# Decoding two float64 weight arrays: eight wide blocks on VectorE and ScalarE in place of sixteen with GpSimd

## The chip, the cores and the metric

The kernel runs on one core of a Trainium2 chip. The metric is the device time of one execution in microseconds (us); the times below are medians over runs. A core has five instruction streams that matter here: PE (TensorE, matmuls), DVE (VectorE), ACT (ScalarE), POOL (GpSimd) and SP (SyncE, which here only issues transfers). Each works through its own list in order and waits for the others by semaphores.

## The reference

Two attentions with a packed set of 32 keys, a dense layer with SoLU and layer norm, and a layer of eight experts with the best one chosen for each token:

```python
p_packed = sm_attn(p, k, v)               # 8 batches x 8 heads, 576 tokens, 64 wide
out = sm_attn(q, p_packed, p_packed)
h = x @ w_in                              # w_in [512, 1024], float64
solu = h * softmax(h)
ln = layer_norm(solu) * g_ln
x = ln @ w_out                            # w_out [1024, 512], float64
...
```

`w_in` and `w_out` arrive as float64, and everything else as float32. The kernel brings the float64 words to the chip as pairs of 32-bit words and makes float32 values of them there.

## The kernel before

The program has two phases. In the first, each of the 8 batches runs through steps that have a letter in the code: P (`packed`: scores of the packed queries, softmax, packed values), S (`scores2`: the tokens' scores against the packed keys), W (`w_keys`: packed values times `w_in`), A (`attnT`: transposed weights), H (`hidden`: a tile of 128 tokens times 1,024 hidden units, max, exp, mean, variance, norm), T (`lnT`: the normed tile transposed and split into a high and a low part, tiles `lh` and `ll`), X (`second`: times `w_out`) and G (`gate`). The second phase runs the experts. From the second batch on, a fixed list of steps overlaps each batch with its neighbours.

Ahead of that list stands a list written out by hand for the first batch. Into it the decoding is mixed: F issues a transfer of raw words, I decodes a block of `w_in`, D a block of `w_out`. A scheduler then orders each engine's instructions, so the order on an engine is not simply that of the list. W needs all of `w_in`; X needs all of `w_out`.

The arrays are cut into 16 blocks of 512 columns (8 of `w_in`, 8 of `w_out`, 512 KB each). The words lie in pairs, lower word first, so that `hi` and `lo` are each every second 32-bit word. A block takes four or five DVE instructions (lines 114 to 117, and 122 for the two blocks whose flag is "n"), one or two ACT instructions (113, 119) and one or two POOL instructions (120, 123). A block of `w_out` takes two more on ACT (154, 155) and one more on POOL (156). The raw words and the scratch words lie in buffers of later tiles (`room`).

Two chains are spoken of below. In H, the max of a tile (`hm`, line 281) lets ACT write `e` (287), then DVE multiplies `e` by the hidden units (289), and this frees the PSUM buffer `h` for the tile after next; there are two such buffers. `e_2` is `e` of tile 2 of batch 0: its line 289 frees the buffer into which PE puts tile 4, `h_4`. After it, ACT squares (292), POOL takes a power (297), and DVE writes the normed tile (298).

## Time and profile before

| | us |
|---|---|
| median of 3 runs | 968.62 |
| lowest and highest | 967.90, 969.72 |
| span of the profiled execution | 967.9 |
| PE busy | 915.5 (95%) |
| DVE busy | 539.3 (56%) |
| ACT busy | 402.2 (42%) |
| POOL busy | 124.2 (13%) |

The profiled execution's own time is the one of 967.90; its span is the same to a tenth, so nothing lies around it. The median is 0.7 us above it. Busy shares are averages over stages: the shares of single stretches are in the rows further down.

### The profile page before, as it was taken

The page shows a single profiled execution, that of the slowest core. Times are in us where ns is not written, and L with a number is a line of the kernel's source. Part 1 is how long each engine was busy: PE and PEld are TensorE (multiplying, and loading weights), DVE is VectorE, ACT ScalarE, POOL GpSimd, SP SyncE. Part 2 cuts the span into 40 slices and gives each one's busy share as a digit, 9 for nine tenths or more (in the row PEclk, how much of TensorE's full clock was granted, in tenths as well). Part 3 has the DMA queues.
Part 4 walks back from the last instruction along what each step waited for, and adds up shares of the span by engine and source line. Part 5 has one row for each costly group of instructions (what it writes and reads, how often), then busy time and mean ns, then how long its engine had stood idle before and what let it go on. Part 6 is the DMA issues. An engine that isn't in the chain of part 4 may idle for free.

```text
span 967.9 us, 18591 instructions
## 1 busy us (share of the span) xinstructions
PE 915.5 (95%) x7480; PEld 807.3 (83%) x7480; DVE 539.3 (56%) x1090; ACT 402.2 (42%) x800; POOL 124.2 (13%) x228
## 2 busy tenths in 40 slices
PE   4466999999999999999999999999999999999997
PEld 1234777887878878788788999999999999999997
DVE  5999758575575756757456243353434353535331
ACT  4447555444554446444345241333323232324230
POOL 2776312011120101101010000000000000000000
PEclk9988999999999999999999999999999999999999
DMA  9613113022221222200106235353535353433411
GB/s 341 244 45 123 50 56 145 14 90 100 102 98 40 82 82 98 99 2 2 50 1 225 78 116 166 99 175 90 182 99 174 102 173 103 149 127 100 132 46 52
DMA packets 42506, 102.89 MB, mean 106 GB/s; under 512 B 4592, under 2 KB 14384, under 8 KB 38320
## 3 DMA queue, kind: packets, MB, share of 16 engines
q1 hardware_dynamic: 42416, 101.65, 31.1%
q8 instruction: 61, 1.00, 0.4%
q14 instruction: 29, 0.24, 0.1%
HBM read 82.60 MB, written 19.04 MB: 105 GB/s over the span
## 4 chain that ended last, share of the span: by engine, by line
PE 87%; DVE 6%; DMA 2%; ACT 1%; issue 1%; SPq 1%; POOL 0%; DVEq 0%; ACTq 0%
PE y L476 21%; PE x L331 21%; PE h L458 21%; PE h L279 11%; PE lt L315 3%; PE wb L218 2%; PE s L170 2%; PE s L231 2%; PE lg L342 1%; PE pp L193 1%; PE at L260 1%; DMA raw_0a<-w 1%; DVE raw L116 1%; PE a1t L184 1%; DVE e L298 1%
## 5 line engine op out<-in xcount | busy, mean ns | idle before, releaser
L331 PE MATMUL x<-lh,wo_hi 128*128 128x320 f32 (+1 forms) x512 | 155.8, 304 | 0.2 <-ACT x L333 0.2
L331 PE MATMUL x<-lh,wo_lo 128*128 128x320 f32 (+1 forms) x512 | 152.5, 298 | 0.0
L331 PE MATMUL x<-ll,wo_hi 128*128 128x320 f32 (+1 forms) x512 | 152.4, 298 | 0.0
L331 PEld LDWEIGHTS x<-lh,wo_hi 128*128 128x128 f32 x512 | 96.7, 189 | 18.6 <-issue 7.4
L331 PEld LDWEIGHTS x<-ll,wo_hi 128*128 128x128 f32 x512 | 96.9, 189 | 3.9 <-issue 2.5
L331 PEld LDWEIGHTS x<-lh,wo_lo 128*128 128x128 f32 x512 | 96.8, 189 | 2.2 <-issue 0.8
L318 DVE TENSOR_TENSOR ll<-lt,lh 128x512 fp32r<-128x512 f32 (+1 forms) x80 | 50.5, 632 | 47.7 <-ACT lh L317 47.6
L279 PE MATMUL h<-wbh,ath 128*128 128x512 f32 (+1 forms) x160 | 68.3, 429 | 6.6 <-DVE e L289 5.9
L281 DVE TENSOR_REDUCE hm<-h 128x1 f32<-128x512 f32 (+1 forms) x80 | 54.3, 685 | 26.2 <-PE h L279 25.7
L279 PE MATMUL h<-wbh,atl 128*128 128x512 f32 (+1 forms) x160 | 65.2, 408 | 0.0
L279 PE MATMUL h<-wbl,ath 128*128 128x512 f32 (+1 forms) x160 | 64.6, 404 | 0.0
L317 ACT CAST lh<-lt 128x512 fp32r<-128x512 f32 (+1 forms) x80 | 43.1, 540 | 46.4 <-PE lt L315 45.8
L489 DVE TENSOR_TENSOR o<-y,gb 128x576 f32<-128x576 f32 (+1 forms) x33 | 24.4, 739 | 67.7 <-PE y L476 65.6
L289 DVE SCALAR_TENSOR_TENSOR e<-e,h 128x1024 f32<-128x1024 f32 (+1 forms) x40 | 48.6, 1215 | 19.9 <-ACT e L287 19.9
L292 ACT ACTIVATE sq<-e,mu 128x1024 bf16<-128x1024 f32 (+1 forms) x40 | 46.0, 1150 | 22.1 <-DVE e L289 17.0
L287 ACT ACTIVATE e<-h,hm 128x1024 f32<-128x1024 f32 (+1 forms) x40 | 44.6, 1115 | 24.8 <-DVE hm L282 24.5
L333 ACT COPY x<-x 128x256 f32<-128x256 f32 (+1 forms) x64 | 25.4, 397 | 62.4 <-PE x L331 62.2
L315 PE MATMUL lt<-ident,e 128*128 128x128 f32 (+1 forms) x320 | 48.5, 271 | 0.9 <-DVE ll L318 0.9
L464 DVE SCALAR_TENSOR_TENSOR hl<-h,hh 128x576 fp32r<-128x576 f32 x64 | 47.8, 749 | 0.3 <-ACT hh L463 0.2
L315 PEld LDWEIGHTS lt<-ident,e 128*128 128x128 f32 (+1 forms) x320 | 35.9, 142 | 9.1 <-issue 4.4
L279 PEld LDWEIGHTS h<-wbh,ath 128*128 128x128 f32 (+1 forms) x160 | 29.8, 186 | 15.5 <-DVE e L289 7.1
L298 DVE TENSOR_SCALAR e<-e,mu,va 128x1024 f32<-128x1024 f32 (+1 forms) x40 | 35.3, 882 | 11.3 <-POOL va L297 10.5
(239 smaller groups left out, 2172.5 us busy)
## 6 DMA issues: line engine op xcount, KB each, us to landing
k<-kT SPq DMA_DIRECT2D x16, 576.0 KB
q<-qT SPq DMA_DIRECT2D x8, 1152.0 KB
x2s<-x SPq DMA_DIRECT2D x8, 1152.0 KB
x<-x2s SPq DMA_DIRECT2D x8, 1152.0 KB
yT<-o SPq DMA_DIRECT2D x31, 288.0 KB
v<-vm SPq DMA_DIRECT2D x8, 1024.0 KB
raw<-w_in SPq DMA_DIRECT2D x8, 512.0 KB
raw<-w_out SPq DMA_DIRECT2D x8, 512.0 KB
```

The source lines that it names most:

```text
L279: T.matmul(ps[:rows, cols], s[x][:, t, g, :rows], s[y][:, g, cols], start=(n == 0), stop=(n == len(passes) - 1))
L281: V.tensor_reduce(nm[:rows, hf : hf + 1], ps[:rows, cols], axis=AX.X, op=ALU.max, negate=True)
L287: A.activation(er, psr, AF.Exp, bias=nm[:rows, 0:1], accum_out=z[:rows])
L289: V.scalar_tensor_tensor(er, er, 1.0 / FF, psr, op0=ALU.mult, op1=ALU.mult, accum_out=mu[:rows])
L292: A.activation(sq[:rows], er, AF.Square, bias=mu[:rows], scale=-float(FF), accum_out=va[:rows])
L298: V.tensor_scalar(er, er, mu[:rows], va[:rows], op0=ALU.add, op1=ALU.mult)
L315: T.transpose(ps[:, fc, :rows], e[:rows, (f0 + fc) * P : (f0 + fc + 1) * P], ident[:rows, :rows])
L318: V.tensor_sub(s["ll", part][:, f0 : f0 + 4, t0 - p0 : t0 - p0 + rows], ps[:, :, :rows], f32(hi))
L331: T.matmul(ps[:, :pn], w[:, fc, cols], s[x, part][:, fc, :], start=(n == 0), stop=(n == 3 * NF - 1))
L458: T.matmul(ps[:, hf, :HALF], w[:, dc, :], x[:, dc, hf * HALF : (hf + 1) * HALF], start=(n == 0), stop=(n == 3 * NC - 1))
L464: V.scalar_tensor_tensor(lo, ps[:, :, :HALF], 0.0, f32(hi), op0=ALU.max, op1=ALU.subtract)
L476: T.matmul(ps[:, hf, :HALF], w[:, fc % 4, :], x[fc][:, hf, :], start=(n == 0), stop=(n == 3 * NF - 1))
```

## The change

Each array is cut into 4 blocks of twice the columns (1,024 columns, 1 MB each): 8 blocks in all. A value is now made as a power of two, taken from the top 16-bit word and left in bfloat16, times the mantissa as a number. A block takes five DVE instructions and one ACT instruction, and a block of `w_out` two ACT scalings, one ACT cast and one DVE subtraction (line 150) more. POOL takes no part. The decoding is done in place in the raw words, with a small 16-bit tile `pw` (two buffers) beside it. The raw words of the first two blocks lie in the buffers of `wbh` and `wbl`, the others in those of `lh`, `ll` and `x2`. The hand-written list is new too.

```diff
-        room = "lh0 ll0 lh1 ll1 e e x2 lh0 ll0 lh1 ll1 e lh1 ll1 x2 lh1".split()
-        by_pool = "yyyyyyyyyynyynyy"
+        room = "wbh wbl lh0 ll0 lh1 ll1 x2 lh1".split()
...
-            lo, hi = w[:, :, 0], w[:, :, 1]
-            a, b2 = t[:, 0], t[:, 1]
-            A.activation(f32(a), f32(hi), AF.Abs)
-            V.tensor_scalar(f32(a), f32(a), F64_LEAST, None, op0=ALU.max)
-            V.tensor_scalar(b2, a, 3, 0x3FFFFFFF, op0=ALU.logical_shift_left, op1=ALU.bitwise_and)
-            V.scalar_tensor_tensor(a, hi, -0x40000000, b2, op0=ALU.bitwise_and, op1=ALU.bitwise_or)
-            V.tensor_scalar(b2, a, -0x800000, None, op0=ALU.bitwise_and)
-            if through_pool:
-                A.activation(f32(lo), lo.bitcast(U32), AF.Copy, scale=2.0**-52)
-                G.tensor_tensor(f32(b2), f32(lo), f32(b2), op=ALU.mult)
-            else:
-                V.scalar_tensor_tensor(f32(b2), lo.bitcast(U32), 2.0**-52, f32(b2), op0=ALU.mult, op1=ALU.mult)
-            G.tensor_tensor(dst, f32(a), f32(b2), op=ALU.add)
+            w = raw.rearrange("p (n w) -> p n w", w=2)
             lo, hi = w[:, :, 0], w[:, :, 1]
+            top = raw.bitcast(U16).rearrange("p (n w) -> p n w", w=4)[:, :, 3]
+            t = p2.tile([P, FF], U16, name=f"pw{i}", tag="pw")
+            V.tensor_scalar(t, top, 0x7FF0, None, op0=ALU.bitwise_and)
+            A.activation(t, t, AF.Relu, bias=mexp, scale=8.0)
+            V.scalar_tensor_tensor(t, top, 0x8000, t, op0=ALU.bitwise_and, op1=ALU.bitwise_or)
+            V.tensor_scalar(hi, hi, 0xFFFFF, 0x100000, op0=ALU.bitwise_and, op1=ALU.bitwise_or)
+            V.scalar_tensor_tensor(f32(lo), lo.bitcast(U32), 2.0**-32, hi, op0=ALU.mult, op1=ALU.add)
+            dst = f32(hi) if dst is None else dst
+            V.scalar_tensor_tensor(dst, f32(lo), 2.0**-20, t.bitcast(BF16), op0=ALU.mult, op1=ALU.mult)
+            return dst
...
-            G.tensor_tensor(wo_lo[:, fc, :], raw, f32(wo_hi[:, fc, :]), op=ALU.subtract)
+            V.tensor_sub(wo_lo[:, 2 * i : 2 * i + 2, :], w, f32(wo_hi[:, 2 * i : 2 * i + 2, :]))
...
-        for step in ("K F0 V F1 F4 F2 F3 F5 P S1 S0 I1 F8 S2 F6 I6 F10 F9 F7 I0 I3 I2 I4 F13 F11 C0 L+ I5 I7 "
-                     "W F12 A0 F14 A1 A2 D0 F15 D1 D2 D3 D4 D5 D7 D6 C1").split():
+        for step in ("K F0 F1 V F2 F3 C0 F4 F5 F6 P S0 S1 S2 I0 I1 I2 I3 W F7 A0 L+ H0 H1 D0 D1 T0 T1 D2 D3 A1 A2 C1").split():
```

SP's list (the transfers) at its start, before: the raw words of one block (`raw<-w_in`) stand ahead of the values and queries of batch 0 (`v`, `q`).

```order
L132 DMA k_130<-kT 128x4x288 x2
L105 DMA raw_133<-w_in 128x512
L138 DMA v_135<-vm 128x2048
L139 DMA v_135<-vt 64x512
L140 DMA q_136<-qT 128x2304
L105 DMA raw_140<-w_in 128x512
```

SP's list at the same place, of the change:

```order
L127 DMA k_132<-kT 128x4x288 x2
L98 DMA raw_135<-w_in 128x1024
L98 DMA raw_137<-w_in 128x1024
L133 DMA v_139<-vm 128x2048
L134 DMA v_139<-vt 64x512
L135 DMA q_140<-qT 128x2304
L98 DMA raw_144<-w_in 128x1024
```

Ahead of `v` and `q` now stand two blocks of twice the size.

DVE's list while the first blocks of `w_in` are decoded, before (`raw` and `bits` are a block's words and scratch, `pn` the packed values of batch 0):

```order
L114 TENSOR_SCALAR bits_143<-bits_143 128x512
L117 TENSOR_SCALAR raw_140<-raw_140 128x512
L115 TENSOR_SCALAR bits_143<-bits_143 128x512
L116 SCALAR_TENSOR_TENSOR bits_143<-raw_142,bits_143 128x512
L114 TENSOR_SCALAR raw_145<-raw_145 128x512
L117 TENSOR_SCALAR bits_143<-bits_143 128x512
L115 TENSOR_SCALAR raw_145<-raw_145 128x512
L114 TENSOR_SCALAR raw_147<-raw_147 128x512
L116 SCALAR_TENSOR_TENSOR raw_145<-raw_145 128x512
L196 TENSOR_TENSOR pn_253<-pp_212,rz_152 128x128
```

DVE's list at the same place, of the change (L111, L113, L114, L115 and L117 are the five DVE lines of the new `decode`, top to bottom):

```order
L113 SCALAR_TENSOR_TENSOR pw_341<-raw_137,pw_341 128x1024
L117 SCALAR_TENSOR_TENSOR w_in_sb<-raw_135,pw_334 128x1024
L168 TENSOR_TENSOR nm_1_187<-nm_1_187 128x1
L114 TENSOR_SCALAR raw_137<-raw_137 128x1024
L115 SCALAR_TENSOR_TENSOR raw_137<-raw_137 128x1024
L174 SCALAR_TENSOR_TENSOR z_1_202<-z_1_202 128x1
L117 SCALAR_TENSOR_TENSOR w_in_sb<-raw_137,pw_341 128x1024
L175 RECIPROCAL rz_156<-z_1_202 128x1
L111 TENSOR_SCALAR pw_348<-raw_144 128x1024
L113 SCALAR_TENSOR_TENSOR pw_348<-raw_144,pw_348 128x1024
L190 TENSOR_TENSOR pn_257<-pp_216,rz_156 128x128
```

Most of the new decode rows take two tensors, and L111 of a block is here followed at once by its L113, between which ACT has to work.

DVE's list up to `e_2`, before; the last of the 16 blocks (`raw_489`) stands right ahead of it:

```order
L298 TENSOR_SCALAR e_1_811<-e_1_811,mu_1_814,va_1_816 128x1024
L282 TENSOR_TENSOR hm_2_842<-hm_2_842 128x1
L281 TENSOR_REDUCE hm_3_873<-h_3_872 128x1
L114 TENSOR_SCALAR raw_489<-raw_489 128x512
L282 TENSOR_TENSOR hm_3_873<-hm_3_873 128x1
L115 TENSOR_SCALAR raw_489<-raw_489 128x512
L116 SCALAR_TENSOR_TENSOR raw_489<-raw_489 128x512
L117 TENSOR_SCALAR raw_489<-raw_489 128x512
L289 SCALAR_TENSOR_TENSOR e_2_858,mu_2_861<-e_2_858,h_2_841 128x1024
L318 TENSOR_TENSOR ll_0_826<-lt_0_0_827,lh_0_825 128x4x128
```

DVE's list up to the same instruction, of the change, where it is on L283:

```order
L150 TENSOR_TENSOR wo_lo<-raw_392,wo_hi 128x1024
...
L312 TENSOR_TENSOR ll_0_499<-lt_0_0_500,lh_0_498 128x4x128
L168 TENSOR_TENSOR nm_1_594<-nm_1_594 128x1
L312 TENSOR_TENSOR ll_0_499<-lt_0_4_507,lh_0_498 128x4x128
L275 TENSOR_REDUCE hm_2_753<-h_2_752 128x1
L174 SCALAR_TENSOR_TENSOR z_1_609<-z_1_609 128x1
L276 TENSOR_TENSOR hm_2_753<-hm_2_753 128x1
L175 RECIPROCAL rz_563<-z_1_609 128x1
L275 TENSOR_REDUCE hm_3_784<-h_3_783 128x1
L276 TENSOR_TENSOR hm_3_784<-hm_3_784 128x1
L283 SCALAR_TENSOR_TENSOR e_2_769,mu_2_772<-e_2_769,h_2_752 128x1024
```

All decode rows still stand ahead of `e_2`, the last of them (L150) 15 rows ahead; two rows of `ll_0` (L312, before L318) have moved to its front. On PE, the packed values of batch 1 (`pp`) have moved behind the first half of `h_4`, and the transposes of tile 1 (`lt_1`) to its front. From the middle of the third batch's W step on, the orders of all engines are the same as before.

## Rows read from the trace of the kernel before

**Rows 1.** Windows: length; busy of PE, PEld, DVE, ACT, POOL; clock; DMA share, GB/s.

```profile
0.00:10.00 10.00, 2.37 (x16) 0.43 (x16) 2.78 (x18) 2.98 (x5) 0.68 (x6) 1.00 0.78 275
10.00:20.00 10.00, 6.94 (x94) 3.84 (x98) 5.71 (x17) 6.36 (x18) 3.05 (x3) 1.00 1.02 392
20.00:90.00 70.00, 38.05 (x317) 22.58 (x306) 67.56 (x112) 37.97 (x76) 51.83 (x44) 0.94 0.44 151
90.00:100.00 10.00, 9.49 (x95) 7.31 (x96) 8.91 (x20) 7.31 (x14) 7.22 (x12) 0.72 0.23 94
110.00:200.00 90.00, 89.75 (x781) 70.50 (x780) 56.42 (x131) 44.94 (x100) 12.13 (x33) 1.00 0.21 69
```

**Rows 2.** The chain of waits, in order of time: start, us, what.

```profile
2.56 6.03 DMA raw<-w_in
...
89.32 1.15 DVE e L289 x2
...
90.51 2.82 PE h L279 x6
```

**Rows 3.** Windows of tiles `raw` and `bits` alone, and the group in both.

```profile
9.00:90.00 81.00, 40.97 (x57) 17.94 (x30) 34.93 (x25) 0.95 0.52 185
...
9.00:90.00 81.00, 9.24 (x12) 2.07 (x3) 8.13 (x6) 0.95 0.52 185
...
L116 DVE SCALAR_TENSOR_TENSOR bits<-raw,bits 128x512 int32<-128x512 int32 x3 | 3.2, 1064 | 0.0
```

**Rows 4.** Timeline of DVE and POOL: start, us, engine, line.

```profile
9.30 0.43 DVE L114 TENSOR_SCALAR raw<-raw 128x512 f32<-128x512 f32 x1 [0.18 <-ACT raw L113]
...
19.75 1.68 DVE L116 SCALAR_TENSOR_TENSOR bits<-raw,bits 128x512 int32<-128x512 int32 x1
...
27.07 0.41 DVE L117 TENSOR_SCALAR raw<-raw 128x512 int32<-128x512 int32 x1
27.40 0.68 DVE L116 SCALAR_TENSOR_TENSOR raw<-raw 128x512 int32<-128x512 int32 x1
...
19.51 1.37 POOL L120 TENSOR_TENSOR raw<-raw 128x512 f32<-128x512 f32 x1 [5.35 <-DVE raw L117]
```

**Rows 5.** Wide DVE work: a group of the whole kernel; line 298 after 110 us, min/median/max.

```profile
L289 DVE SCALAR_TENSOR_TENSOR e<-e,h 128x1024 f32<-128x1024 f32 x32 | 38.9, 1217 | 17.5 <-ACT e L287 17.5
...
L298 DVE TENSOR_SCALAR e<-e,mu,va x35: 794/812/816, 134.0 to 521.1; 128x1024 f32<-128x1024 f32 x28, 64x1024 f32<-64x1024 f32 x7
```

**Rows 6.** Timeline of DVE, rows outside the decoding.

```profile
46.78 0.94 DVE L243 TENSOR_SCALAR z<-z 128x16 f32<-128x16 f32 x1
...
48.08 1.01 DVE L243 TENSOR_SCALAR z<-z 64x8 f32<-64x8 f32 x1
...
71.06 0.15 DVE L282 TENSOR_TENSOR hm<-hm 128x1 f32<-128x1 f32 x1
...
73.65 1.25 DVE L282 TENSOR_TENSOR hm<-hm 128x1 f32<-128x1 f32 x1
...
81.73 1.64 DVE L298 TENSOR_SCALAR e<-e,mu,va 128x1024 f32<-128x1024 f32 x1
...
84.04 1.55 DVE L298 TENSOR_SCALAR e<-e,mu,va 128x1024 f32<-128x1024 f32 x1
```

**Rows 7.** Two groups up to 110 and 100 us, and a row of DVE's timeline.

```profile
L245 POOL TENSOR_TENSOR a<-a,z 128x512 f32<-128x512 f32 x4 | 4.4, 1089 | 3.2 <-PE wb L218 1.9 <-DVE z L244 1.3
...
L318 DVE TENSOR_TENSOR ll<-lt,lh 128x512 fp32r<-128x512 f32 x4 | 2.7, 687 | 0.7 <-ACT lh L317 0.7
...
49.72 1.16 DVE L115 TENSOR_SCALAR raw<-raw 128x512 int32<-128x512 int32 x1
```

**Rows 8.** Timeline of ACT and PE.

```profile
71.24 1.12 ACT L287 ACTIVATE e<-h,hm 128x1024 f32<-128x1024 f32 x1 [1.37 <-DVE hm L282]
...
84.12 1.04 PE L315 MATMUL lt<-ident,e 128*128 128x128 f32 x8
...
85.97 1.73 PE L193 MATMUL pp<-v,a1T 128*32 128x64 f32 x80 [0.80 <-ACT a1T L185]
```

More of the change, by code (lines that the diff above doesn't have):

```diff
@@ L57, in fused_kernel @@
     V.memset(mhalf, -0.5)
+    mexp = const.tile([P, 1], F32, name="mexp")
+    V.memset(mexp, -8.0 * 16 * 896)
     eidx = const.tile([1, B], I32, name="eidx")
@@ L108, in decode @@
[L108 to L123 removed]
+            pool = pa if room[i][0] == "w" else p1
@@ new lines, in fetch, with decode @@
+            raw = pool.tile([P, 2 * FF], I32, name=f"raw{i}", tag=room[i])
+            SY.dma_start(raw.bitcast(I64) if len(src.shape) == 2 else raw.bitcast(I64).rearrange("p (f n) -> p f n", f=src.shape[1]), src)
+            return raw
+        def decode(i, raw, dst):
+            w = raw.rearrange("p (n w) -> p n w", w=2)
+            lo, hi = w[:, :, 0], w[:, :, 1]
+            top = raw.bitcast(U16).rearrange("p (n w) -> p n w", w=4)[:, :, 3]
[8 more added lines that the diff above has]
+            return dst
@@ L144, in load, with decode_w_in, decode_w_out @@
             load_vq(b)
[L146 to L156 removed]
+        def decode_w_in(c, raw):
+            decode(c, raw, w_in_sb[:, c, :])
+        def decode_w_out(i, raw):
+            w = decode(4 + i, raw, None).rearrange("p (f n) -> p f n", f=2)
+            for k in range(2):
+                fc = 2 * i + k
+                A.activation(w[:, k], w[:, k], AF.Copy, scale=g_sb[:, fc : fc + 1])
+            A.copy(wo_hi[:, 2 * i : 2 * i + 2, :], w)
+            V.tensor_sub(wo_lo[:, 2 * i : 2 * i + 2, :], w, f32(wo_hi[:, 2 * i : 2 * i + 2, :]))
         def packed(b):
```

28 lines of the change are left out of this document (3 added, 25 removed).

## The prediction

> **What bounds the kernel now.** I read the windows first. From 110 to 200 us PE is busy 89.75 of 90 us, so once it has come that far only less work could help it. From 20 to 90 us it is busy 38.05 of 70, and DVE 67.56 of 70 [rows 1]: there DVE's list, in its fixed order, sets the pace. PE's idle time up to 90 us is 90 - 2.37 - 6.94 - 38.05 = 42.6 us. The chain of waits shows where this ends: line 289 of `e_2` is done at about 90.5, and at 90.51 PE starts `h_4`, for which that row freed the buffer [rows 2]. From there PE is 9.49 of 10 us busy. So I ask one thing: how much earlier does DVE reach the end of `e_2`? PE's work behind it is the same but for some steps moved across, and the orders soon are the same, so the end of the kernel moves with it.
>
> Then I looked at what DVE does there. All 66 decode rows stand ahead of `e_2`. In the windows of the tiles they take 40.97 + 9.24 - 3.2 = 47.0 us (3.2 us lie in both) [rows 3]. Much of it isn't work: line 116 takes 0.68 us at 27.40 and 1.68 at 19.75, where POOL has had a multiply running since 19.51 for 1.37 us [rows 4]. Such a row of DVE ends only once POOL is through. Rows that aren't decoding suffer too: line 282, 0.15 us at 71.06, takes 1.25 at 73.65 [rows 6].
>
> **The change, term by term,** in DVE time up to the end of `e_2`, start to start (a row overlaps the next by 0.07: 27.07 + 0.41 is 27.48, and the next starts at 27.40 [rows 4]).
>
> 1. Removed: 66 rows, 47.0 us, in which their overlaps with one another are already out. For their overlaps with other rows I take 0.05 a row, 3.3 in all: -43.7.
>
> 2. Added: 44 rows, all ahead of `e_2`: 8 x 5, and 4 subtractions (line 150) that POOL did before. 24 rows take two tensors (lines 113, 115, 117), as line 289 does at the same width for 1.217 us [rows 5]; so do the 4 subtractions: 28 x 1.217 = 34.1. 16 rows take one tensor (lines 111, 114). At 512 columns such a row takes 0.41 against 0.68 with two tensors [rows 4], though its fixed part must be as large: two columns at a time. From 512 to 1,024 columns two-tensor rows grow by 1.217 - 0.68 = 0.54, so these should grow by 0.27 to 0.68: 16 x 0.68 = 10.9. With overlaps out, 45.0 - 44 x 0.07 = 41.9: +41.9. Line 298, one tensor wide with two column operands, takes 0.81 [rows 5], which would add 2.1. No row shows a one-tensor row on every second word or every fourth half word, as lines 111 and 114 read; bounds are 0.41 (half the width) and 1.217 (one column at a time). I take 0.68, because line 116, which reads `hi` at every second word, at 0.68 loses nothing against row groups on dense words (0.687, line 318 [rows 7]).
>
> The Trainium skill (Vector Engine (DVE) Microarchitecture Reference, 5.1 Performance modes) names no step as a condition for running one-tensor rows two at a time between SBUF tiles; by it lines 111 and 114 stay at the dense rate, which gives the sum that I use. The same page (5.2 Measured stream behaviour on trn2) speaks against this change: a port keeps its rate only on runs of two adjacent words, and a source that hops at every word cost 1.73 instead of 1.05 ns a column there. By that figure 24 two-tensor rows would take 0.73 us more each, an estimate of +17.5 us; line 116 at 0.68 does not bear it out for one such input.
>
> 3. Delays that POOL's decode work put on other rows: line 298 of `e_0` and `e_1` 1.64 and 1.55 instead of 0.81, two rows of line 282 about 1.25 instead of 0.15, one of line 243 0.94 instead of 0.15 [rows 5, 6]: 0.83 + 0.74 + 2.2 + 0.79 = 4.6. I leave out smaller ones: -4.4, start to start.
>
> 4. Delays that stay: POOL's three softmax multiplies (1.09 us [rows 7]). Before, one met line 243 (1.01 at 48.08 [rows 6], 0.85 lost), and one a decode row (1.16 at 49.72 [rows 7], in term 1). Now nearly every row between is a decode row of the kind that waits, so all three are paid: 3 x 1.05 - 0.85 = +2.3.
>
> 5. Two rows of `ll_0` (0.687 [rows 7]) now stand ahead of `e_2`: +1.2.
>
> 6. Start: the first block, 512 KB asked for at 2.56, is there after 6.03 us, at 8.6 [rows 2], and DVE's first decode row starts at 9.30, after an ACT row [rows 4]. A block of 1 MB takes 512 KB / 392 GB/s [rows 1] = 1.3 us longer, but DVE needs no ACT first: first row at 9.95, +0.65. That two blocks stand ahead of `v` and `q` makes these some 4 us later; `v` is needed only after two softmaxes, and DVE has block 1 to decode meanwhile: nothing on the path.
>
> 7. Idle time of DVE: before, 4.29 from 10 to 20 and 2.44 from 20 to 90 [rows 1], 6.7. Now: twice a block's line 113 stands right behind its line 111 with ACT's row between (1.12 at this width, as line 287 [rows 8], and 0.15 for the two handovers), 2.5. After `e_0` most decode work is gone, and DVE waits for PE, ACT and POOL in turn: I reckon 2.5, what 20 to 90 us had. 5.0 in all: -1.7.
>
> Up to `e_2`: -43.7 + 41.9 - 4.4 + 2.3 + 1.2 + 0.65 - 1.7 = -3.75.
>
> 8. PE behind that point: `pp` of batch 1 (1.73) now stands behind the first half of `h_4`, and the eight transposes of tile 1 (1.04) in front [rows 8]: +0.7. DVE has no more POOL delays from 90 to 100 us, where PE idled 0.51 [rows 1]: -0.5. The granted clock was 0.72 there [rows 1], part of the time at 1.2 GHz after a wait of PE; PE waits in the same way ahead of `h_4` now, so I leave it: 0.
>
> Costs of nothing: ACT loses far more than it gains and was busy 37.97 of 70 us [rows 1], which hides its rows. The last block's transfer (`raw_392`) waits on SP for line 150 of the block whose buffer it takes, and behind it stand the keys of batch 2, needed only in that batch's first step. DVE's line 111 for it stands seven rows behind that line 150: about 6 us against 2.7 of transfer and the issue. If that cover fails, DVE stands still for the difference, a microsecond or two.
>
> Sum: -3.75 + 0.7 - 0.5 = -3.55, so 967.9 - 3.55 = 964.35 for an execution like the profiled one; the median of the runs shown is 0.7 above it: **965.0 us**.
>
> **Rivals.**
> - *One column at a time* (slower). If lines 111 and 114 lose the double rate on strided words, 16 rows cost 1.217 instead of 0.68: +8.6, 973.6. For it: no row shows a stepped one-tensor row. Against: line 116's unhurt step. It turns the sign above 0.68 + 3.55/16 = 0.90 us a row.
> - *Three stepped streams* (slower). Line 115 reads `lo` and `hi` and writes `lo`, all at every second word; line 116 had one stream like it. At half rate its eight rows cost 1.07 us more each (1,024 columns at 1.04 ns): +8.5, 973.5. If all 24 two-tensor rows ran at half rate, it would be +25.7. (It is what the Trainium skill says in 5.2 of the page named above, in the one place where the rows leave room for it.)
> - *Nothing shows.* DVE is relieved, but between `e_0` and `e_2` the chain through PE's `h_2`, ACT and POOL sets the pace, and DVE only idles more: 968.6. For it: after `e_0` only one decode row is left in DVE's list. Against: DVE idled 2.44 us in 70 [rows 1].
> - *More than the sum.* Adding the new list row by row from 9.95, with its waits, brings me to `e_2` at 84 to 85 instead of 90.5; and if PE comes to `h_4` at 2.4 GHz, the 10 x (1 - 0.72) = 2.8 us that the lower clock cost from 90 to 100 [rows 1] are saved too: 968.6 - 5.5 - 2.8, about 960.5.
>
> **How the numbers follow.** No change means within 0.2% (1.9 us), about what a measurement of this kernel can tell: 966.7 to 970.6. The sum's case has 0.48 (own range 961.5 to 968.5; 0.38 of it faster, 0.10 same), more than the sum 0.12 (faster), nothing shows 0.14 (same), one column at a time 0.12 and three stepped streams 0.14, of which 0.02 ends within the bounds. So faster 0.50, same 0.26, slower 0.24. The range goes from 959.5 to 974.0: below it lies some of the fourth rival, above it the far form of the second and what comes with either, some 0.15 together.
>
> **What would show it.** Lines 111 and 114 near 0.68 us, lines 113, 115 and 117 near 1.2. POOL nearly empty from 10 to 90 us. Line 282 and line 298's successors without rows over 1 us but beside the three softmax multiplies. `e_2` done at about 86.7 and PE busy from there. Wrong would make it: wide rows far above 1.2 us, long DVE idle between 10 and 35 us (transfers or ACT), or DVE idle after `e_0` of 5 us and more.

## The result, and the profile after

The changed kernel takes 957.05 us (median of 4 runs, 956.84 to 957.72), the one before 968.26 on the same chip (4 runs, 967.7 to 969.72): a ratio of 0.9878, 95% interval 0.9865 to 0.9892. It is 1.2% faster, by more than three times what the prediction said (11.9 us between the two profiled spans, 967.9 and 956.0, against 3.55), and the median lies below the predicted range.

One number of the prediction's base needs a word. In the changed kernel's profiled execution 1.7 us lie around the span (957.72 against 956.0), and it is nearly so in every run below; the profiled execution before was therefore more likely the one of 969.72 than that of 967.90. The forecast of the median stays where it was (969.72 - 3.55 - 1.1 = 965.1), and from here on spans are compared with spans.

The windows of the changed kernel, the stretches of [rows 1]: length; busy of PE, PEld, DVE, ACT, POOL with their instructions; clock; DMA share, GB/s. The last row is DVE alone, from its first decode row to the end of `e_2`.

```profile
10.00:20.00 10.00, 3.97 (x24) 1.66 (x24) 8.80 (x14) 4.40 (x10) 0.00 (x0) 1.00 1.02 391
20.00:90.00 70.00, 48.30 (x419) 30.38 (x419) 65.26 (x109) 38.57 (x69) 13.60 (x19) 0.78 0.45 163
90.00:100.00 10.00, 10.00 (x133) 8.76 (x132) 9.35 (x22) 6.12 (x13) 2.13 (x5) 1.00 0.24 72
...
10.19:82.77 72.58, 68.24 (x111) 0.79 0.53 196
```

The same window of DVE alone in the kernel before, up to its own end of `e_2`:

```profile
9.30:90.51 81.21, 74.44 (x131) 0.95 0.52 185
```

From 20 to 90 us POOL is busy 13.60 us instead of 51.83 and PE 48.30 instead of 38.05 (in part because its clock there is 0.78 and not 0.94: the same matmul is busy for longer); DVE is nearly as full as it was, 65.26 instead of 67.56. Its list up to `e_2` takes 72.58 us instead of 81.21, with 68.24 busy instead of 74.44 in 111 instructions instead of 131. From 90 to 100 us PE has no idle time and a clock of 1.00, where before it was 9.49 busy at 0.72 [rows 1].

The chain of waits around the end of `e_2`: start, us, what.

```profile
70.97 4.73 PE h L273 x12
...
77.83 2.77 PE h L273 x12
...
80.63 0.70 DVE hm L275
...
81.51 1.22 DVE e L283 x2
82.73 0.04 issue
82.77 1.59 PE h L273 x6
84.37 1.66 PE pp L187 x80
86.03 0.67 PE x L325 x4
```

The place is the one that the prediction names, DVE's last row of `e_2` and behind it `h_4`, but it comes at 82.77 instead of 90.51 [rows 2], and PE does the first six matmuls of `h_4` in 1.59 us, which took 2.82. The same view shows the two levels of the clock: twelve matmuls of a tile take 4.73 us at 70.97, behind a long wait of PE, and 2.77 at 77.83. The first X matmul, behind `h_4`'s first half and `pp`, starts at about 86 us (85.96); before it started at 99.23. PE's timeline of the changed kernel and of the one before:

```profile
85.96 0.38 PE L325 MATMUL x<-lh,wo_hi 128*128 128x256 f32 x1
...
99.23 0.36 PE L331 MATMUL x<-lh,wo_hi 128*128 128x256 f32 x1
```

One thing more stands in this chain: the matmuls of `h_2` (70.97) and `h_3` (77.83) are right ahead of DVE's last rows, and DVE waits for `h_3`. Its timeline:

```profile
80.63 0.69 DVE L275 TENSOR_REDUCE hm<-h 128x1 f32<-128x512 f32 x1 [0.30 <-PE h L273]
```

So from about 71 us on DVE's list is not alone in setting the pace.

DVE's groups from 9 to 91 us: line, operation, tiles, shapes, count; busy, mean ns; idle time ahead and what ended it.

```profile
L115 DVE SCALAR_TENSOR_TENSOR raw<-raw 128x1024 f32<-128x1024 uint32 x8 | 9.7, 1214 | 0.1
L113 DVE SCALAR_TENSOR_TENSOR pw<-raw,pw 128x1024 uint16<-128x1024 uint16 x8 | 9.7, 1207 | 2.2 <-ACT pw L112 2.2
L114 DVE TENSOR_SCALAR raw<-raw 128x1024 int32<-128x1024 int32 x8 | 5.4, 681 | 0.0
L111 DVE TENSOR_SCALAR pw<-raw 128x1024 uint16<-128x1024 uint16 x8 | 5.4, 681 | 1.0 <-DMA raw<-w_in 1.0
...
L117 DVE SCALAR_TENSOR_TENSOR w_in_sb<-raw,pw 128x1024 f32<-128x1024 f32 x4 | 4.9, 1218 | 0.0
L150 DVE TENSOR_TENSOR wo_lo<-raw,wo_hi 128x1024 fp32r<-128x1024 f32 x4 | 4.8, 1208 | 0.0
...
L292 DVE TENSOR_SCALAR e<-e,mu,va 128x1024 f32<-128x1024 f32 x4 | 3.2, 812 | 1.4 <-POOL va L291 1.4
```

One-tensor rows on every second word (L114) and every fourth half word (L111) take 0.681 us; two-tensor rows take 1.21, also L115 with all its streams at every second word. L292, whose two ahead of `e_2` took 1.64 and 1.55 [rows 6], is at 0.81.

Rows of the changed kernel's timeline: start, us, engine, line, tiles, and the idle time ahead in brackets.

```profile
42.94 1.00 DVE L237 TENSOR_SCALAR z<-z 128x16 f32<-128x16 f32 x1
...
47.23 0.92 DVE L237 TENSOR_SCALAR z<-z 64x8 f32<-64x8 f32 x1
...
42.08 1.83 POOL L239 TENSOR_TENSOR a<-a,z 128x512 f32<-128x512 f32 x1 [40.78 <-DVE z L238]
46.90 1.22 POOL L239 TENSOR_TENSOR a<-a,z 128x512 f32<-128x512 f32 x1 [2.99 <-DVE z L238]
50.13 4.29 POOL L239 TENSOR_TENSOR a<-a,z 64x256 f32<-64x256 f32 x1 [2.01 <-ACT pw L112]
...
82.77 0.45 PE L273 MATMUL h<-wbh,ath 128*64 128x512 f32 x1 [0.76 <-DVE e L283]
83.06 0.39 PE L273 MATMUL h<-wbl,ath 128*64 128x512 f32 x1
...
101.53 1.09 PE L212 MATMUL wb<-w_in_sb,ppc 64*32 64x512 f32 x16
```

And of the kernel before, the first two matmuls of `h_4` (the second answers to the one at 83.06) and one of the four groups of eight for batch 1, two of which stand as one row at 101.53 above:

```profile
90.51 0.69 PE L279 MATMUL h<-wbh,ath 128*64 128x512 f32 x1 [2.81 <-DVE e L289]
91.00 0.63 PE L279 MATMUL h<-wbl,ath 128*64 128x512 f32 x1
...
104.19 1.06 PE L218 MATMUL wb<-w_in_sb,ppc 64*32 64x512 f32 x8
```

The only two DVE rows outside the decoding that POOL still stretches are the two of L237. POOL's own multiplies are the stretched ones now: 4.29 us for the smallest of them. PE waits 0.76 us ahead of `h_4` instead of 2.81, and comes to it at 2.4 GHz.

### The profile page after: what moved, and what is told of

The parts are those of the page before. It is cut to its first block, busy times and chain, and to the rows that moved or that the text cites. A ratio compares the mean times of both kernels' runs of the same rounds, so it can differ in the third digit from the quotient of the medians.

```text
span 956.0 us, 18453 instructions
## 1 busy us (share of the span) xinstructions
PE 911.4 (95%) x7480; PEld 806.0 (84%) x7480; DVE 531.5 (56%) x1069; ACT 393.0 (41%) x774; POOL 74.3 (8%) x190
## 4 chain that ended last, share of the span: by engine, by line
PE 89%; DVE 6%; DMA 2%; ACT 1%; issue 1%; SPq 0%; ACTq 0%; DVEq 0%
PE x L325 22%; PE y L468 21%; PE h L450 21%; PE h L273 11%; PE lt L309 3%; PE wb L212 2%; PE s L225 2%; PE lg L336 2%; PE s L164 2%; PE pp L187 1%; PE at L254 1%; DVE raw L115 1%; DVE pw L113 1%; DMA raw<-w_in 1%; DMA raw_0a<-w 1%
## 5 line engine op out<-in xcount | busy, mean ns | idle before, releaser
L312 DVE TENSOR_TENSOR ll<-lt,lh 128x512 fp32r<-128x512 f32 (+1 forms) x80 | 50.4, 631 | 43.1 <-ACT lh L311 43.0
L283 DVE SCALAR_TENSOR_TENSOR e<-e,h 128x1024 f32<-128x1024 f32 (+1 forms) x40 | 48.6, 1216 | 21.1 <-ACT e L281 21.1
L455 ACT ACTIVATE hh<-h 128x576 fp32r<-128x576 f32 x64 | 41.3, 647 | 0.0
L292 DVE TENSOR_SCALAR e<-e,mu,va 128x1024 f32<-128x1024 f32 (+1 forms) x40 | 32.3, 807 | 11.1 <-POOL va L291 10.4
```

What stands on the lines that cost most here:

```text
L283: V.scalar_tensor_tensor(er, er, 1.0 / FF, psr, op0=ALU.mult, op1=ALU.mult, accum_out=mu[:rows])
L312: V.tensor_sub(s["ll", part][:, f0 : f0 + 4, t0 - p0 : t0 - p0 + rows], ps[:, :, :rows], f32(hi))
```

## The experiments

"Pinned" below means that every instruction of an engine is chained to the one ahead of it, so that the scheduler can't choose another order (`order` lists the instructions, engine by engine):

```diff
+        for k in order:
+            if k != 65535 and last is not None:
+                tc.add_manual_dep(seq[k], seq[last].name, mybir.DependencyInfo(mybir.DependencyClass.NoSync, mybir.DependencyReason.DATA))
+            last = None if k == 65535 else int(k)
```

Several kernels that were not pinned came out in an order of their own; where that decides the reading, it is said. Ratios are against the kernel before on the same chip, whose median was between 969.2 and 969.5 in these sets.

### The kernel before without POOL, and without POOL's work

```diff
-        by_pool = "yyyyyyyyyynyynyy"
+        by_pool = "n" * 16
...
-            G.tensor_tensor(dst, f32(a), f32(b2), op=ALU.add)
+            V.tensor_tensor(dst, f32(a), f32(b2), op=ALU.add)
...
-            G.tensor_tensor(wo_lo[:, fc, :], raw, f32(wo_hi[:, fc, :]), op=ALU.subtract)
+            V.tensor_sub(wo_lo[:, fc, :], raw, f32(wo_hi[:, fc, :]))
```

> The kernel before with GpSimd taken off its decode work and nothing else: 16 blocks of 512 columns, the old arithmetic; the 16 additions, the 14 products that GpSimd did and the 8 subtractions now stand in DVE's list. My theory: POOL's rows cost DVE waiting time, and it is the shorter arithmetic together with POOL's absence that brings the gain, neither of them alone. In the trace of before, 66 decode rows take 48.5 us, 17.7 more than the same rows at the shortest duration of their form, and other rows 3.7 more: 21.4 us of waiting to be freed. Added are 38 two-tensor rows of 512 columns, 0.68 - 0.07 = 0.61 each: 23.2 us. So the end of e_2 stays within 3 us of 90.5 and the kernel at 965 to 972 us. Rival, that POOL's removal is the gain by itself: e_2 near 83, some 958 to 961 us.

964.33 us (963.37 to 964.53), ratio 0.9952, interval 0.9935 to 0.9969. `e_2` is done at 90.2, as before: all but two of DVE's 104 decode rows stand ahead of it, so DVE does nearly all of POOL's work in the time in which it waited for POOL. Yet the kernel is faster, just below the range expected, and PE's list came out otherwise. Its timeline:

```profile
87.92 0.38 PE L331 MATMUL x<-lh,wo_hi 128*128 128x256 f32 x1 [1.03 <-DVE ll L318]
...
90.26 0.45 PE L279 MATMUL h<-wbh,ath 128*64 128x512 f32 x1
```

X work fills what was PE's wait, and `h_4` comes without a wait and at 2.4 GHz (0.29 us from its first matmul to the next at 90.55, before 0.49). The end of `e_2` alone does not give the time.

Next, POOL's product, sum and subtraction left out, with copies on ACT so that all else stays (what is lost of the weights is the lower word's part, and the low half of `w_out`; the number that sends the experts into further passes is held at 0):

```diff
-                G.tensor_tensor(f32(b2), f32(lo), f32(b2), op=ALU.mult)
...
-            G.tensor_tensor(dst, f32(a), f32(b2), op=ALU.add)
+            if dst is not None:
+                A.copy(dst, f32(a))
...
-            G.tensor_tensor(wo_lo[:, fc, :], raw, f32(wo_hi[:, fc, :]), op=ALU.subtract)
```

> The kernel before with POOL's decode work left out and DVE's 66 decode rows kept: the product with the mantissa, the addition and the subtraction for wo_lo are not computed (ACT copies the word with sign and exponent instead, wo_lo is zero, and the loop over the remaining experts is held at no pass). Theory: DVE's rows fall to their unhurt durations, 0.41 for lines with one tensor and 0.68 for those with two; the decode rows' sum falls from 48.5 to about 31 us, and e_2 ends 15 to 20 us earlier unless PE's and ACT's chain from h_0 to e_2 sets the pace first: 948 to 956 us. Rival, that the stretched rows of before had another cause (the steps of two words, the transfers): the sum stays above 42 us and the time at 962 to 970.

956.4 us (955.97 to 957.81), ratio 0.9878, interval 0.9862 to 0.9895, just above the range expected. With the same DVE rows `e_2` is done at 72.6, 18 us earlier: about what the 66 decode rows of the kernel before take above the shortest of their form (17.7 of their 48.5 us). So POOL's work held DVE's decoding up by 18 us. The total gains 13.7 in the span and not 18: behind X, PE idles 3.2 us from 110 to 300 us here, where it idled 0.55 before, in an order that differs up to batch 5.

### POOL beside the new decoding

Twelve products on POOL that nobody reads, behind the first three blocks of `w_in`; all other engines' orders are those of the changed kernel, row for row.

```diff
-            decode(c, raw, w_in_sb[:, c, :])
+            decode(c, raw, w_in_sb[:, c, :]); [G.tensor_tensor(scr, w_in_sb[:, c, :512], w_in_sb[:, c, 512:], op=ALU.mult) for _ in range(4 if c < 3 else 0)]
```

> The changed kernel with twelve products of 128 x 512 added on POOL, four behind each of the first three blocks of w_in, into a tile that nobody reads; DVE's order is the same, row for row. POOL alone needs 12 x 1.09 = 13.1 us for them, beside the decode rows from about 18.6 us on. Theory, that DVE's two-tensor rows keep the path and only one-tensor rows wait: the rows of lines 111 and 114 beside them grow, those of lines 113, 115 and 117 stay below 1.3, POOL's rows take 2 us and more, DVE loses 1 to 3 us in all: 957 to 960 us. Rival, that POOL holds DVE up as in the kernel before, 0.39 us per us of POOL or more, or one whole row each: DVE loses 5 to 13 us, 962 to 970 us.

966.26 us (9 runs, 965.56 to 967.25), ratio 0.9971, interval 0.9961 to 0.9981; span 964.6, 8.6 above the changed kernel's. The timeline of POOL and DVE:

```profile
18.85 14.76 POOL L142 TENSOR_TENSOR scr<-w_in_sb 128x512 f32<-128x512 f32 x8 [17.55 <-DVE nm L168]
...
19.47 2.17 DVE L115 SCALAR_TENSOR_TENSOR raw<-raw 128x1024 f32<-128x1024 uint32 x1
21.57 1.23 DVE L174 SCALAR_TENSOR_TENSOR z<-z 128x1 f32<-128x1 f32 x1
22.71 1.21 DVE L117 SCALAR_TENSOR_TENSOR w_in_sb<-raw,pw 128x1024 f32<-128x1024 f32 x1
...
23.92 1.68 DVE L111 TENSOR_SCALAR pw<-raw 128x1024 uint16<-128x1024 uint16 x1
```

Each side waits for the other. A POOL row takes 14.76 / 8 = 1.85 us instead of 1.09 [rows 7]; of DVE, L115 loses 0.96, a row of one column (L174) 1.08, L117 then nothing, L111 1.0. `e_2` comes 9.1 us later (91.8) and X 9.1 later (95.05): 0.76 us of DVE for each of the twelve rows, passed on to the end but for 0.5 us. The theory that a two-tensor row keeps its way beside POOL falls (L115).

### One part of the change undone: the subtractions on POOL

```diff
-            V.tensor_sub(wo_lo[:, 2 * i : 2 * i + 2, :], w, f32(wo_hi[:, 2 * i : 2 * i + 2, :]))
+            G.tensor_tensor(wo_lo[:, 2 * i : 2 * i + 2, :], w, f32(wo_hi[:, 2 * i : 2 * i + 2, :]), op=ALU.subtract)
```

> The changed kernel with one part undone: the four subtractions for wo_lo (128 x 1024) go back to POOL. DVE loses four rows of 1.21 - 0.07, 4.6 us ahead of e_2. Theory, that DVE's two-tensor rows, one close behind the other, keep the path and POOL waits: POOL's rows take 2.5 to 5 us, DVE's others lose 1 to 2 us in all, e_2 ends 2 to 4 us earlier, 953 to 956 us. Rival, that POOL holds DVE up as it did before (0.39 us of DVE for each us of POOL's rows, or the whole row where DVE comes second): four rows of 2.2 us cost DVE 3.5 to 8 us, e_2 at the same place or later, 956 to 961 us.

967.1 us (10 runs, 965.97 to 968.45), ratio 0.9982, interval 0.9973 to 0.9992. It says little by itself, since the scheduler gave another order up to batch 4: `e_2` is done at 82.9 and X starts at 84.87, no later than in the changed kernel, and the time goes behind that. The window from 150 to 200 us:

```profile
150.00:200.00 50.00, 47.84 (x388) 36.40 (x387) 32.39 (x79) 24.25 (x54) 6.91 (x17) 0.93 0.19 65
```

PE idles 2.2 us there, and its clock is 0.93. So the same edit again, the other engines pinned to the changed kernel's order:

> The four subtractions for wo_lo on POOL once more, now with every engine's order pinned to that of the changed kernel (each row is chained to the one ahead of it, POOL's as in the first such run), since the run without pins came out with another order up to batch 4. DVE has four rows of 1.14 us less ahead of e_2, 4.6 us. Theory, that the first run lost its time by its order behind batch 0 and not by POOL: POOL's rows of 2.2 to 3 us cost DVE 3 to 6 us, so e_2 ends within 1.5 us of 82.7 and the kernel takes 955 to 959 us. Rival, that POOL's four rows themselves cost the 10 us: 963 to 968 us again.

962.9 us (961.61 to 964.52), ratio 0.9933, interval 0.9917 to 0.995; span 961.2, 5.2 above the changed kernel's and between the two ranges expected. `e_2` is done at 86.7, 4.0 later, though DVE has four rows fewer (4.6 us); X starts at 91.29. DVE and POOL in the timeline:

```profile
48.74 3.13 POOL L150 TENSOR_TENSOR wo_lo<-raw,wo_hi 128x1024 fp32r<-128x1024 f32 x1 [0.89 <-ACT wo_hi L149]
...
49.64 0.63 DVE L214 TENSOR_TENSOR wbl<-wb,wbh 128x512 fp32r<-128x512 f32 x1
50.19 2.75 DVE L117 SCALAR_TENSOR_TENSOR raw<-raw,pw 128x1024 f32<-128x1024 f32 x1
...
65.42 2.81 DVE L114 TENSOR_SCALAR raw<-raw 128x1024 int32<-128x1024 int32 x1
...
79.36 2.40 DVE L292 TENSOR_SCALAR e<-e,mu,va 128x1024 f32<-128x1024 f32 x1
```

Each subtraction stretches one DVE row by 1.5 to 2.1 us (also L111 at 56.59 to 2.54), where the same subtraction on DVE costs 1.21. The row at 49.64, which reads PSUM, is not stretched. PE waits 2.06 us ahead of `h_4`, and the clock is 0.89 and 0.94 in the windows of 80 to 90 and 90 to 100 us. These four subtractions on POOL cost more of DVE's time than they take on DVE; in the kernel before, by the first experiment, the two were about equal.

### Another part undone: wide rows

The five DVE rows and the ACT row of a block cut into two halves of 512 columns:

```diff
-            V.tensor_scalar(t, top, 0x7FF0, None, op0=ALU.bitwise_and)
+            for h in range(2):
+                n = slice(h * 512, h * 512 + 512)
+                V.tensor_scalar(t[:, n], top[:, n], 0x7FF0, None, op0=ALU.bitwise_and)
...
```

> The changed kernel with every decode row cut in two, of 512 columns each (40 rows become 80; the four subtractions stay whole): only the width is undone. By the durations of the rows at 512 columns, 0.41 for one tensor and 0.68 for two, less the overlap of 0.07: 32 x 0.34 + 48 x 0.61 = 40.2 us against 16 x 0.61 + 24 x 1.14 = 37.1, 3.1 us more ahead of e_2, of which a microsecond may come back since ACT's first half is done earlier: e_2 at 84.5 to 86, 958.5 to 961 us. Rival, that the wide rows are most of the gain: 964 us and more.

969.64 us (10 runs, 969.34 to 972.66), ratio 1.0007, interval 0.9998 to 1.0017. All of the gain is gone, but again not where the halves are: `e_2` is done at 83.4, and the order differs up to batch 7 (PE idles 3.6 us from 110 to 300 us and 52.4 in all, as in the kernel before). With the order pinned to the changed kernel's:

> The decode rows cut in two once more, now with the order of the changed kernel pinned, the two halves of a row one behind the other. Theory, that the width is worth the fixed part of 40 more rows, 3.1 us by their durations at 512 columns, and that the first such run lost the other 9 us by its order: e_2 at 84.5 to 86 and 958 to 961 us. Rival, that the narrow rows lose more than their durations say: 964 us and more.

959.0 us (958.76 to 959.25), ratio 0.9893, interval 0.9877 to 0.991; span 957.0, `e_2` at 83.8, X at 87.11. Two of its groups of DVE from 9 to 91 us (its L118 and L117 are L115 and L114 of the changed kernel):

```profile
L118 DVE SCALAR_TENSOR_TENSOR raw<-raw 128x512 f32<-128x512 uint32 x16 | 10.3, 684 | 0.0
L117 DVE TENSOR_SCALAR raw<-raw 128x512 int32<-128x512 int32 x16 | 6.0, 419 | 0.0
```

Twice 684 is 1.37 against 1.21 us, twice 419 is 0.84 against 0.68; part of it vanishes in shorter waits for ACT (0.7 against 2.2 us ahead of the row that answers to L113). Width is worth 1 to 2 us of the 12. The order alone, in the run before, cost another 10.

What the new arithmetic is worth can be read beside this. Start to start, decoding takes DVE 52.2 us in 104 rows in the first experiment (old arithmetic, no POOL), 45.6 in 84 rows with halves and pinned, and 41.6 in 44 rows in the changed kernel. So some 6.6 us of DVE's list go with the arithmetic and 3.9 with the width, while POOL's absence alone left `e_2` where it was. The first experiment has an order of its own, and no run has the new arithmetic with nothing else changed, so this split is read and not shown.

### The clock at `h_4`

Four products on POOL behind `e_1`, meant to hold `e_2` back and to let PE wait longer:

```diff
-            s["ln", t] = e
+            s["ln", t] = e; [G.tensor_tensor(scr, er[:, :512], er[:, 512:], op=ALU.mult) for _ in range(4 if (b, t) == (0, 1) else 0)]
```

> The changed kernel with four products of 128 x 512 added on POOL behind the normalisation of e_1 (they read e_1, nobody reads them): they run beside DVE's rows just ahead of e_2. The order of every other row on every engine is the same. It asks what a late e_2 costs when everything ahead of it is in time. Each such row cost DVE 0.8 us in the run with twelve of them, so e_2 ends about 3.2 us later, 85.9, and PE's wait ahead of h_4 grows from 0.76 to about 3.9 us, more than the 2.81 of the kernel before. Theory, that this wait is what put h_4 and the transposes behind it at 1.2 GHz before: h_4's steps are 0.43 instead of 0.23, which costs 2 to 3 us more: 957 + 3.2 + 2.5, 961.5 to 964 us. Rival, that the clock has nothing to do with this wait: h_4 stays at 0.23, 959.5 to 961 us.

957.86 us (957.8 to 959.46), ratio 0.9888, interval 0.9871 to 0.9904. `e_2` stayed at 82.8 instead of the 85.9 expected: most of DVE's rows beside these products read PSUM (lines 312, 275, 283) and kept their 0.68 and 1.22 us, and only one-column rows grew, two of them to 0.51 and 0.53. PE waited 1.72 us and still came at 2.4 GHz. As a test of the clock it is inconclusive. The other way round, in the kernel before with its order pinned: ten products of identities on PE in the gap ahead of `h_4`.

```diff
+            [T.matmul(ps[:, 384:512], ident, ident, start=True, stop=True) for _ in range(10 if b == 1 else 0)]
```

> The kernel before, its order pinned, with ten products of the identity with itself (128 x 128) put on PE behind pp of batch 1, in the time in which PE waits 2.81 us for e_2; nobody reads them. Nothing else is changed. Theory, that this wait puts the first half of h_4 and the transposes behind it at 1.2 GHz and that this cost 2 to 3 us of the kernel before: h_4's steps are 0.23 instead of 0.43, 965 to 967 us against 969. Rival, that the clock falls for another reason or costs nothing: 968 to 971 us.

967.81 us (10 runs, 967.33 to 968.77), ratio 0.9987, interval 0.9977 to 0.9997; span 965.6. Its windows of 80 to 90 and 90 to 100 us, and the first row of `h_4`:

```profile
80.00:90.00 10.00, 9.09 (x129) 7.56 (x127) 9.69 (x18) 8.09 (x20) 7.22 (x8) 1.00 0.26 85
90.00:100.00 10.00, 9.36 (x113) 7.56 (x114) 9.96 (x22) 8.18 (x15) 8.28 (x14) 1.00 0.19 78
```

And PE's timeline:

```profile
90.09 0.45 PE L279 MATMUL h<-wbh,ath 128*64 128x512 f32 x1 [0.41 <-DVE e L289]
```

PE idles 0.41 us instead of 2.81 ahead of `h_4`, the clock is 1.00 instead of 0.94 and 0.72, and X starts 2.1 us earlier (97.17), of which 0.4 is an earlier end of `e_2` (90.0). So the lower clock behind that wait cost the kernel before some 1.3 (by the ratio) to 1.7 us (by the trace), 1.6 by the medians (969.45 and 967.81); the interval goes from 0.3 to 2.2 us. The time lies between the two ranges expected.

### The order of the start, and of what stands ahead of X

First, the first block's transfer ahead of the keys:

```diff
-        for step in ("K F0 F1 V F2 F3 ...
+        for step in ("F0 K F1 V F2 F3 ...
```

> The changed kernel with the first block of w_in asked for ahead of the keys of batch 0 (two words of the hand-written order change places). DVE's list sets the end of e_2, so an earlier start moves it: the block is there some 2.7 us earlier (1 MB instead of a place behind 1.2 MB of keys), DVE's first decode row starts near 6.5 to 7.5 instead of 10.19, and the softmax rows that wait for the keys stand 2 to 3 us later, behind block 0. Theory: e_2 ends 1.5 to 3 us earlier, 953.5 to 956 us. Rival, that the softmax chain through PE and ACT (first P step, then S and W) is as tight as DVE's list: what DVE gains at the start it waits for between 15 and 40 us, and the time stays at 956 to 959 us.

969.95 us (10 runs, 967.45 to 971.12), ratio 1.0002, interval 0.9992 to 1.0011, outside both ranges. The order differs up to batch 4, and PE idles 4.6 us from 110 to 300 us, so the total tells little; DVE's start tells more:

```profile
5.84 0.69 DVE L111 TENSOR_SCALAR pw<-raw 128x1024 uint16<-128x1024 uint16 x1 [3.94 <-DMA raw<-w_in]
7.75 1.23 DVE L113 SCALAR_TENSOR_TENSOR pw<-raw,pw 128x1024 uint16<-128x1024 uint16 x1 [1.22 <-ACT pw L112]
...
22.21 0.68 DVE L111 TENSOR_SCALAR pw<-raw 128x1024 uint16<-128x1024 uint16 x1
```

DVE starts 4.35 us earlier than in the changed kernel (10.19) and has lost it all by the third block, whose L111 starts at 22.21 here and at 21.85 there: it waits for ACT and for the scores. So the later start of the change is not what holds it up here.

Then the packed values of batch 1 (`pp`) put earlier in the hand-written list:

```diff
-  ... W F7 A0 L+ H0 H1 D0 D1 T0 T1 D2 D3 A1 A2 C1
+  ... W F7 A0 L+ H0 H1 A1 P+ D0 D1 T0 T1 A2 H2 D2 H3 D3 C1
```

> The changed kernel with batch 1's first step (P) and the steps H2 and H3 placed earlier in the hand-written order, ahead of the last blocks of w_out. PE waits 5.71 us from 65.3 on for ACT's exponentials of that step, which stand behind those of h_0 and h_1, and falls to 1.2 GHz for h_2 and h_3. With the transposes of that step ahead of h_2 and DVE's list one row shorter ahead of e_2, I expect e_2 0 to 2 us earlier, 954 to 957 us. Rival, that DVE's list alone sets the end of e_2 and the new order only moves the waits: 956.5 to 960 us.

959.07 us (957.27 to 959.78), ratio 0.9891, interval 0.9875 to 0.9908, in the rival's range. `e_2` comes at 81.8, but PE waits 1.69 us for ACT (`ath`) ahead of `h_4`, and X starts at 85.69, as in the changed kernel (85.96). Two more orders of the changed kernel, with the edit of the pinned kernels alone and lists written by hand, bring `e_0`, `e_1` and `e_2` forward. In the first, DVE's rows for them stand ahead of the last blocks of `w_out`, and `h_2`'s first half on PE ahead of the transposes of batch 1's weights (`a1t`):

> The changed kernel with the same rows, pinned in an order written from the trace: the maxima of h_0 and h_1 (lines 275 and 276) and both rows of line 283 stand ahead of the rows of the last two blocks of w_out (line 150 of the third, lines 114 to 117 of the fourth) instead of behind them, ACT's exponentials and squares likewise ahead of the scaling of the last block, and PE's first half of h_2 ahead of the transposes of batch 1. In the changed kernel PE is idle from 63.9 to 69.6 since h_2 and h_3 need the buffers that line 283 frees at 70.1 and 71.2. By the rows' durations line 283 of e_0 now ends at 66.1 and e_2 at 77.6 instead of 82.7, while the last decode row stays near 80. Theory: PE's idle time up to 83 falls by 3 to 5 us, 951 to 955 us. Rival, that X, which needs all of the decoding, starts no earlier, and PE only waits later: 955.5 to 958 us.

956.67 us (956.28 to 957.25), ratio 0.9867, interval 0.985 to 0.9883: not to be told from the changed kernel (0.9865 to 0.9892), as the rival had it. No version here clearly beats it, the one that leaves POOL's work out aside. `e_0` and `e_1` are done at 66.5 and 68.2 instead of 70.2 and 71.3, `e_2` at 81.3 instead of 82.7 (77.6 was expected), X starts at 84.86. So 3.7 and 3.1 us ahead of `e_2` were worth 1.4 at its end. The second goes further the same way:

> The changed kernel with all its rows in a second order written from the traces: as in the first such order, and on PE h_2 and h_3 whole, one behind the other, right behind s of batch 1, then the transposes of both tiles and h_4, and X ahead of the rest of batch 1's first step (the second half of its transposes and pp); on DVE the last two rows of line 150 behind those of line 312 that X reads first, on ACT the exponentials of e_2 and e_3 ahead of the scaling of the last block. By durations e_2 ends near 75 and X starts at 80.5 to 82.5 instead of 85.96, with pp (1.7 us) behind it: 952 to 955.5 us. Rival, that X then waits for the last blocks of w_out (fc 4 to 7) or PE for batch 1 behind it: 955.5 to 959 us.

964.74 us (964.31 to 966.19), ratio 0.9954, interval 0.9937 to 0.997, outside both ranges. `e_2` is done at 76.8, 5.9 us earlier than in the changed kernel, and the kernel takes 7.7 us longer. In PE's timeline `h_4`'s second half waits for a max (`hm`) that this order puts late in DVE's list, and then runs at 1.2 GHz:

```profile
87.96 0.69 PE L273 MATMUL h<-wbh,ath 128*64 128x512 f32 x1 [4.52 <-DVE hm L275]
```

In the trace X stands behind this half and behind `pp` (at 91.93), not ahead of `pp` as was meant; it starts at 93.59. In the changed kernel its first four matmuls stand ahead of the second half. Last, the kernel before without POOL (the edit of the first experiment), now with PE, ACT and SP pinned to the order of before:

> The kernel before with POOL's decode work on DVE, now with PE's, ACT's and SP's order pinned to that of the kernel before (DVE's own order is the scheduler's up to batch 0's last tile, then that of before). In the run without pins X stood ahead of h_4 on PE and filled its wait for e_2. Theory, that the 4.9 us of that run came from this order and POOL's absence alone is worth little as long as DVE has to do its work: e_2 at 89 to 92, PE waits 2 us and more ahead of h_4, 966 to 971 us. Rival, that POOL's absence is worth the 5 us by itself: 962 to 965 us again.

965.09 us (964.66 to 966.4), ratio 0.9958, interval 0.9943 to 0.9972. `e_2` is done at 82.4, which neither theory had: DVE's list, left free, put decode rows behind it. PE and DVE:

```profile
91.61 3.44 PE L231 MATMUL s<-bd,q 128*64 128x64 f32 x64 [3.52 <-issue]
...
90.93 0.58 DVE L205 TENSOR_SCALAR bd<-ppT 64x128 f32<-64x128 f32 x2
```

PE waits 3.52 us ahead of the scores of batch 1 (`s`), whose operand `bd` DVE has ready at 91.51, behind decode rows. These scores then take 3.44 us, with a granted clock of 0.61 from 92.0 to 95.4, where they took 2.08 in the kernel before, and X starts behind them at 95.40. PE idles 4.2 us from 80 to 90 us. `e_2` is 8 us earlier than in the first experiment, the gain is the same. Both orders without POOL gain 4 to 5 us, so the first experiment's gain is not only its order's. How it splits between the two isn't settled.

The start of X sums these runs up. For the kernels whose order behind it is that of the changed kernel (or of before):

| kernel | `e_2` done | X starts | span | span less start of X |
|---|---|---|---|---|
| changed, another order (first of two) | 81.3 | 84.86 | 955.5 | 870.6 |
| changed | 82.7 | 85.96 | 956.0 | 870.0 |
| changed, four POOL products behind `e_1` | 82.8 | 86.07 | 956.1 | 870.0 |
| changed, halves, pinned | 83.8 | 87.11 | 957.0 | 869.9 |
| changed, subtractions on POOL, pinned | 86.7 | 91.29 | 961.2 | 869.9 |
| changed, another order (second) | 76.8 | 93.59 | 962.5 | 868.9 |
| changed, twelve POOL products | 91.8 | 95.05 | 964.6 | 869.6 |
| before, no POOL, pinned | 82.4 | 95.40 | 963.1 | 867.7 |
| before, PE kept at work | 90.0 | 97.17 | 965.6 | 868.4 |
| before | 90.4 | 99.23 | 967.9 | 868.7 |

The last column moves by 3 us over a range of 14 in the start of X; the end of `e_2` sets the time only where X follows it closely. The kernels left out (the first two of before, and the unpinned ones with their own order) have 871.6 to 881.4 there: they lose behind X.

## Why the prediction was wrong in size

The direction and the place were right, and so was the mechanism in the main: DVE's list up to `e_2` sets the pace, POOL's rows stretch DVE's, and the end moves with what PE does behind `e_2`. That it moves with `e_2` itself held for this pair of orders and not for those tried later. Two terms failed, and they carry 6.9 of the 8.3 us by which the sum fell short (-11.88 against -3.55); decoding and idle time add 0.9 and 0.8, and the start takes 0.2 back. To set the trace against the prediction's steps, each DVE row is counted to the start of the next, idle time apart.

1 and 2, decoding: predicted -43.7 + 41.9 = -1.8, measured 44.36 before and 41.64 after, -2.7. The assumed 0.68 and 1.217 us are there as 0.681 and 1.207 to 1.218. With that both slower rivals fall: *one column at a time* wanted 1.217 for L111 and L114, *three stepped streams* 2.3 for L115. The Trainium skill (Vector Engine (DVE) Microarchitecture Reference, 5.2 Measured stream behaviour on trn2), by whose figure the two-tensor rows would have taken some 0.70 us more each (1,024 columns at 1.73 instead of 1.05 ns, an estimate; the prediction has 0.73), is not borne out for hops of one word: L115's 1.214 is the dense rate.

3 and 4, other rows, **the first failed step**: predicted -4.4 + 2.3, measured -4.65 (all rows outside the decoding 30.08 before and 26.63 after, a fall of 3.45 that has the +1.2 of step 5 in it). Step 3 was about right for two of its three groups, and too small by one that it left out: line 282 and its successor L276 from 2.56 to 0.38, line 298 and L292 from 3.04 to 1.45, the other maxima of the packed scores (L166, L168) 0.7 less. Step 4 failed: "Now nearly every row between is a decode row of the kind that waits, so all three are paid", +2.3. For the rows of line 243 and the decode rows beside them steps 3 and 4 had -0.79 + 2.3 = +1.5 together; the three rows of L243 took 2.36 and those of L237 take 1.84, -0.5, and the decode rows lose nothing. Only two rows of L237 were stretched, by about 0.85 and 0.8, and the decode rows beside the three multiplies keep their 0.68 and 1.21: POOL waits there, up to 4.29 us for one row. The experiment with twelve added POOL products shows what the sum missed: both engines wait, and which of them does is not fixed. There a POOL product cost DVE 0.76 us on average; here the last of the three multiplies cost it nothing.

5: +1.2 as predicted. 6: +0.89 instead of +0.65; in the run with the early first block a start 4.35 us earlier was used up by the third block, so this term need not reach the end. 7: idle 6.77 before and 4.31 after, -2.5 instead of -1.7. ACT's rows ahead of L113 cost 2.2 of it (2.5 was reckoned), and no row waits for the last block of `w_out`, so that cover held.

Up to `e_2` this is -7.74 instead of -3.75. The step by step walk through the list under the rival *more than the sum* (84 to 85) was nearer than the sum (86.7); the end came at 82.7.

8, PE behind it, **the second failed step**: predicted +0.7 - 0.5 + 0 = +0.2, measured -4.1 (126.27 us before and 122.13 after, from the start of `h_4` to the matmul at 216.78 and 204.90, from which the two run alike). Counted to the next row's start: `h` -2.1, `lt` -1.7, `wb` -2.0, `pp` +1.7, idle +0.3, small ones -0.3. The clock's part of it was left at "0" because "PE waits in the same way ahead of `h_4` now". It doesn't: the wait is 0.76 us and not 2.81, and PE is at 2.4 GHz from 77 us on. The run with PE kept at work shows that part by itself, some 1.3 to 1.7 us, below the 2.8 that the rival had. `wb` is an order that the prediction didn't look at: in the changed kernel two groups of eight matmuls for the two halves of the partitions stand next to each other and take 1.02 us together (101.53 to 102.55), and two more of the next batch again at 152.35; before each of a batch's four groups had its own 1.0 (104.19 to 105.19). That it is this which saves the 2.0 us is read from the trace; no run tried it alone. Of `lt`, some 0.8 are eight transposes fewer in the stretch; the rest is the clock and the order.

-7.74 - 4.14 is the 11.9 of the spans. *Nothing shows* falls as well, with 11.9 us. But the chain that it named, through PE's `h_2`, is what the chain of waits shows for 70.97 to 80.6 us of the changed kernel: after `e_0` DVE waits 2.0 us for ACT, POOL and PE, near the 2.5 reckoned in step 7.

What would have made step 4 right stood in the trace of the kernel before: POOL's rows of one and the same kind were unequal, 1.37 us at 19.51 [rows 4] and here 1.96.

```profile
53.62 1.96 POOL L120 TENSOR_TENSOR raw<-raw 128x512 f32<-128x512 f32 x1 [0.59 <-issue]
```

So POOL was waiting too, and a collision charged to DVE in full counts as DVE's a wait that can be POOL's.
